# Performer attention with a hard-swish layer on one core: bfloat16 transposes for the second batch, another load order, and another rank for the first batch's second half

## The chip, the cores and the metric

The kernel runs on one core of one Trainium2 chip. The metric is device time in microseconds. The core has five engines that run side by side, each with its own stream of instructions: TensorE (PE in the profile; its weight loads are PEld), VectorE (DVE), ScalarE (ACT), GpSimd (POOL) and SyncE (SP), which here only issues transfers. Engines wait for each other through semaphores.

## The reference

Eight batches of eight heads with 576 tokens of width 64 go through an attention with random features, and its result through a two-layer network with a hard-swish gate.

```
def phi(x):
    proj = einsum('bhsd,md->bhsm', x, omega)
    sq = sum(x * x, axis=-1) / 2
    h = proj - sq
    h = h - max(h, axis=-1)
    return exp(h) / sqrt(m)
q_p, k_p = phi(q * scale), phi(k * scale)
kv  = einsum('bhsm,bhsd->bhmd', k_p, v)
z   = sum(k_p, axis=2)
num = einsum('bhsm,bhmd->bhsd', q_p, kv)
den = einsum('bhsm,bhm->bhs', q_p, z) + 1e-06
x   = (num / den)            # 4608 tokens x 512
h   = x @ w_in               # 512 -> 2048
g   = h * clip(h + 3, 0, 6) / 6
out = g @ w_out              # 2048 -> 512
```

The maximum is over the 128 features of each token. For q every factor that belongs to a token alone falls out of num / den. For k the factor 1 / max stays, and the kernel multiplies it into v.

## The kernel before

**Work of one batch.** A batch has four pairs of heads. Of the 576 tokens of a head, 512 are its main rows and 64 its leftover rows; all leftovers of a batch are handled together. For each batch, `attention(b)` does the following.

- `turns` transposes k and q in chunks of 128 x 128 on TensorE (operations `T`), and ScalarE or VectorE copies the result out of PSUM into `kT` and `qT` (`Tev`). This holds for batches 0 and 1 (`PE_T = 2`); later batches use DMA transposes issued by SP.
- `K`: TensorE projects k onto omega (L634), ScalarE takes the exponential (L640), VectorE the maximum over features (L643).
- `Q`: the same projection for q (L651) and exponential (L655), without a maximum.
- `pair(b, m, t)`: for a pair of heads VectorE takes the reciprocals (L735), VectorE or GpSimd multiplies v by them (`vc`, L739; `vcl`, L674, is the same for the leftover rows), TensorE forms `kv` (L752, L754), a copy brings it to SBUF as `kvz`, TensorE forms `num` (L775), VectorE divides (L787, L791).
- `turn_x` transposes the quotient (`X`) and copies it into `xT`, again on TensorE for batches 0 and 1 and by DMA for later ones. Batch 0 does this by halves of a pair (A and B), so that the first half of block 0 can begin early.

Block `blk` of the network is the 512 main tokens' worth of batch `blk`; a ninth block holds the leftovers of all batches (`xS`). `mm1` multiplies by `wi` (L843, for block 0 `mm1_half`, L868, in two halves A and B of tokens), ScalarE and VectorE form the gate (`relu`, L849 or L877; `g`, L851 or L879), and `mm2` multiplies by `wo` (L901). The `g` operation frees the PSUM bank.

**The two ways to transpose on TensorE.** The helper `turn` (L421) uses the transpose instruction with a bfloat16 result in PSUM for batch 0 (L423), and an ordinary matmul by the identity with a float32 result for batch 1 (L424). `turned` gives the view of the result, and the cost that the planner assumes for the copy is `both(n, 2)` for batch 0 and `both(n, 1)` for batch 1.

**What sets the order.** Operations are declared with a list of possible engines, an assumed duration, what they read and write, and a priority (smaller is sooner). `Prog.schedule` then plans all engines at once with these assumed durations: it picks an engine and a PSUM bank (eight banks, the ring) for each operation, and the order on each engine. `Prog.emit` writes the instructions in that order with the waits that remain. So a changed duration or priority can move instructions anywhere on any engine. `by_path` sets priorities: every operation that a goal depends on gets `base` minus 0.02 times its distance from the goal. It is called for the first matmuls of block 0's second half, `mm1.0B.0` (base -0.3), and then of its first half, `mm1.0A.0` (base -1.0). Since the operations of `mm1_half` are tied to each other in a chain by the key `"mm1"`, those of half A are among what `mm1.0B.0` depends on.

**Fillers.** While TensorE would have nothing to do at the start, the planner puts in matmuls on a constant tile (`idle`, L461).

**Loads.** Batch 0 is loaded in float32 (L495) by SP and ACT in the order of `FIRST`; ("k", 1) are k's main rows in four transfers, ("k", 0) its leftover rows in one. ScalarE, VectorE or GpSimd cast k and q to bfloat16. GpSimd issues the loads of w_in (L471) in four pieces, the first once the first piece of v has landed, and after them the loads of batch 1, w_out (L477), and so on; each of these is held back by a gate, an earlier transfer or a later matmul.

Of the kernel before, what the change touches and what calls it, by code (L numbers as in the profile page):

```python
# [41 lines left out]
class Prog:  # L42
# [8 lines left out]
    def op(self, eng, occ, emit, prio, reads=(), writes=(), alloc=(), lat=0.2, group=None, inc=1, name="", slack=0.0, dslack=0.0, issue=0.5, spare=0, packet=46.0):  # L51
        o = Op()
        o.engs = (eng,) if isinstance(eng, str) else tuple(eng)
        o.eng = None
        o.emit, o.occ, o.lat, o.prio, o.name = emit, occ, lat, prio, name
        o.alloc = list(alloc)
        o.group, o.inc, o.slack, o.dslack, o.issue, o.spare, o.packet = group, inc, slack, dslack, issue, spare, packet
        o.seq = len(self.ops)
        deps = {}
        virts = []  # L60
        for kx in reads:
            for d in self.w.get(kx, ()):
                deps[d] = True
            self.r.setdefault(kx, []).append(o)
            if isinstance(kx, Virt):
                virts.append(kx)
        for kx in writes:
            for d in self.r.get(kx, ()):
                if d is not o:
                    deps.setdefault(d, False)  # L70
            for d in self.w.get(kx, ()):
                deps.setdefault(d, False)
            self.w[kx] = [o]
            self.r[kx] = []
            if isinstance(kx, Virt):
                virts.append(kx)
        for vx in set(virts):
            vx.users.append(o)
            vx.left += 1
        o.virts = list(set(virts))  # L80
        o.deps = deps
        o.succ = []
        o.end = o.start = None
        o.emitted = None
        self.ops.append(o)
        return o

    def by_path(self, goals, base, scale):

        far = {o: 0.0 for o in goals}  # L90
        for o in reversed(self.ops):
            if o not in far:
                continue
            for d in o.deps:
                occ = min(d.occ.values()) if isinstance(d.occ, dict) else d.occ
                t = far[o] + occ + d.lat
                if t > far.get(d, -1.0):
                    far[d] = t
        for o, t in far.items():
            if o not in goals and o.prio > -8:  # L100
                o.prio = base - scale * t

    def schedule(self):
# [211 lines left out]
def _emit(nc, es, q, k, v, omega, w_in, w_out, out):  # L315
# [14 lines left out]
    HALVES = [(0, 2), (2, 4)]  # L330
    SPLIT = 3
    LATE = 0.4
    FIRST = [("k", 1), ("q", 1), ("k", 0), ("v", 0), ("v", 1), ("q", 0)]
    REST = [("k", 1), ("k", 0), ("q", 1), ("q", 0), ("v", 0), ("v", 1)]
    W_GATE = [("v32", 0, 1), ("v32", 0, 3), ("v32", 1, 3), ("v32", 1, 3)]
    alpha = float(D) ** -0.25
# [3 lines left out]
    EV_T = ("DVE", "ACT")  # L340
# [78 lines left out]
        return f  # L419

    def turn(E, vx, b, i, src):  # L421
        if b == 0:
            return E.transpose(ringb[vx.slot][:, 128 * i:128 * i + 128], src, ident[:])  # L423
        return E.matmul(ring.t[vx.slot][:, 128 * i:128 * i + 128], src, ident[:], start=True, stop=True)  # L424

    def turned(vx, b, n):
        return ringb[vx.slot][:, 0:n] if b == 0 else ring.t[vx.slot][:, 0:n]


    op("SP", 0.2, lambda E: E.dma_start(om32[:], omega), -9.8, writes=["om32"], group="dom", inc=16, lat=1.8,  # L430
# [109 lines left out]
    def attention(b):  # L540
# [30 lines left out]
        def turns(t, name, dbl, dst, src, p):  # L571
            vT = Virt(ring)
            n = 128 * len(dbl)

            def e_T(E):
                for i, x in enumerate(dbl):
                    ins = turn(E, vT, b, i, src[:, 2 * x:2 * x + 2, :].rearrange("p c d -> p (c d)"))
                return ins

            op("PE", len(dbl) * (0.057 if b else 0.06), e_T, p, reads=rows_of(t, dbl) + ["ident"],  # L580
               writes=[vT], alloc=[vT], lat=0.25, slack=sl, dslack=2 * sl, spare=sp, name="T%s%d.%s" % (t, b, name))
            op(EV_T if b else T0, both(n, 1 if b else 2), evac(lambda: dst, lambda: turned(vT, b, n).rearrange(
                "p (j t) -> p j t", j=dst.shape[1])),
               p, reads=[vT], writes=[(t + "T", x) for x in dbl], name="Tev%s%d.%s" % (t, b, name))

# [141 lines left out]
    def pair(b, m, t):  # L727
# [66 lines left out]
        def turn_x(i0, i1, part):  # L794
            vx = Virt(ring)
            n = 128 * (i1 - i0)
            pt = "" if len(part) > 1 else "AB"[part[0]]

            def e_x(E):
                for i in range(i0, i1):  # L800
                    ins = turn(E, vx, b, i - i0, xb[pb][:, m, 128 * i:128 * i + 128])
                return ins

            op("PE", (i1 - i0) * (0.057 if b else 0.06), e_x, t + 0.03, reads=[("xb", pb, m, x) for x in part] +
               ["ident"], writes=[vx], alloc=[vx], lat=0.25, slack=sl, spare=sp, name="X" + nm + pt)
            op(EV_T, both(n, 1 if b else 2), evac(lambda: xT[pb][:, m, 128 * i0:128 * i1], lambda: turned(vx, b, n)),
               t + 0.03, reads=[vx], writes=[("xT", pb, m, x) for x in part], name="Xev" + nm + pt)

        if b == 0:
# [189 lines left out]
```

## Time and profile before

| | us |
|---|---|
| median of five runs | 326.21 |
| lowest and highest | 325.78, 326.45 |
| the profiled execution | 325.78 |
| its span | 324.0 |
| TensorE busy in the span | 318.4 |
| VectorE, ScalarE, GpSimd busy | 208.6, 189.3, 78.5 |

How to read it: the span is the time between the first and the last instruction that the profiler saw. "Busy" counts an engine's instructions, fillers too. A timeline row gives the start, how long the row lasts, the engine, the line, the operation with its tiles and how many instructions the row holds; in brackets is the idle time of the engine before it and what ended that. A row of the waits gives the waiting engine and line, what it waited for, the total, the number of times and the longest one, in us. Matmuls overlap, so 42 of them take far less than 42 times the duration of one.

### The profile page before, as it was taken

The page shows a single profiled execution, that of the slowest core. Times are in us where ns is not written, and L with a number is a line of the kernel's source. Part 1 is how long each engine was busy: PE and PEld are TensorE (multiplying, and loading weights), DVE is VectorE, ACT ScalarE, POOL GpSimd, SP SyncE. Part 2 cuts the span into 40 slices and gives each one's busy share as a digit, 9 for nine tenths or more (in the row PEclk, how much of TensorE's full clock was granted, in tenths as well). Part 3 has the DMA queues.
Part 4 walks back from the last instruction along what each step waited for, and adds up shares of the span by engine and source line. Part 5 has one row for each costly group of instructions (what it writes and reads, how often), then busy time and mean ns, then how long its engine had stood idle before and what let it go on. Part 6 is the DMA issues. An engine that isn't in the chain of part 4 may idle for free.

```text
span 324.0 us, 5914 instructions
## 1 busy us (share of the span) xinstructions
PE 318.4 (98%) x2263; PEld 175.0 (54%) x2263; DVE 208.6 (64%) x463; ACT 189.3 (58%) x386; POOL 78.5 (24%) x110
## 2 busy tenths in 40 slices
PE   8999999999999999999999999999999999999996
PEld 6678865545554545555455545555555444444443
DVE  4869886698576938865687468756865354433411
ACT  3968981598387519755876377647674353444400
POOL 2725643057051502620244032402010000000000
PEclk9999999999999999999999999999999999999999
DMA  7999999989980999799629974996012201000024
GB/s 248 245 196 163 267 169 183 255 140 141 230 197 1 148 142 282 106 218 164 180 31 165 186 222 50 166 207 212 14 53 58 74 7 59 32 34 32 32 67 97
DMA packets 89516, 44.33 MB, mean 137 GB/s; under 512 B 56080, under 2 KB 85008, under 8 KB 89488
## 3 DMA queue, kind: packets, MB, share of 16 engines
q1 hardware_dynamic: 62272, 30.85, 42.0%
q0 software_dynamic: 26512, 12.46, 31.7%
q10 hardware_dynamic: 704, 0.66, 0.6%
q8 instruction: 18, 0.29, 0.4%
q14 instruction: 10, 0.08, 0.1%
HBM read 36.73 MB, written 9.44 MB: 143 GB/s over the span
## 4 chain that ended last, share of the span: by engine, by line
PE 93%; DVE 1%; issue 0%
PE p L901 38%; PE p L843 34%; PE p L651 4%; PE p L868 4%; PE p L634 4%; PE p L775 3%; PE p L752 2%; PE p L424 1%; PE p L754 1%; PE p L423 0%; DVE mx L643 0%; PE p L688 0%; DVE vc L739 0%; DVE xb L791 0%; DVE kvz L411 0%
## 5 line engine op out<-in xcount | busy, mean ns | idle before, releaser
L901 PE MATMUL p<-wo,gT 128*128 128x512 bf16 (+2 forms) x592 | 141.8, 373 | 0.0
L851 DVE SCALAR_TENSOR_TENSOR gT<-tsb,p 128x512 bf16<-128x512 bf16 x128 | 86.5, 683 | 53.4 <-ACT tsb L849 52.7
L849 ACT ACTIVATE tsb<-p 128x512 bf16<-128x512 f32 x128 | 76.9, 605 | 68.8 <-PE p L843 67.6
L843 PE MATMUL p<-xT,wi 128*128 128x512 bf16 x448 | 108.4, 379 | 0.0
L901 PEld LDWEIGHTS p<-wo,gT 128*128 128x128 bf16 x592 | 55.9, 98 | 55.5
L843 PEld LDWEIGHTS p<-xT,wi 128*128 128x128 bf16 x448 | 42.6, 98 | 45.4
L643 DVE TENSOR_REDUCE mx<-kp 128x4 f32<-128x512 bf16 x72 | 47.4, 675 | 15.5 <-ACT kp L640 15.3
L640 ACT ACTIVATE kp<-p 128x512 bf16<-128x512 f32 x72 | 40.9, 613 | 13.6 <-PE p L634 13.6
L655 ACT ACTIVATE qpT<-p 128x512 bf16<-128x512 f32 (+1 forms) x80 | 40.8, 579 | 3.3 <-PE p L651 3.3
L739 POOL TENSOR_TENSOR vc<-v,cc 128x512 bf16<-128x512 f32 x23 | 25.1, 1091 | 44.1 <-DVE cc L735 29.1
L791 DVE TENSOR_TENSOR xb<-p,rec 128x384 bf16<-128x384 f32 (+1 forms) x64 | 28.5, 476 | 0.0
L634 PE MATMUL p<-om,kT 128*128 128x256 bf16 x144 | 23.5, 273 | 0.1
L651 PE MATMUL p<-qT,om 128*128 128x512 bf16 (+1 forms) x80 | 22.9, 358 | 0.0
L410 ACT COPY osb<-p 128x512 f32<-128x512 f32 x26 | 15.3, 588 | 9.2 <-PE p L901 9.2
L674 POOL TENSOR_TENSOR vcl<-vl,cc 64x260 bf16<-64x260 f32 x8 | 5.0, 624 | 60.3 <-DVE cc L670 50.8
L411 DVE COPY osb<-p 128x512 f32<-128x512 f32 (+2 forms) x11 | 7.1, 643 | 18.7 <-PE p L901 18.7
L634 PEld LDWEIGHTS p<-om,kT 128*128 128x128 bf16 x144 | 13.2, 98 | 9.3 <-ACT kT L410 0.6
L775 PEld LDWEIGHTS p<-kvz,qpT 128*128 128x128 bf16 x312 | 13.9, 98 | 7.1 <-DVE kvz L411 0.6
L843 PE MATMUL p<-xS,wi 128*128 128x512 bf16 x64 | 16.4, 379 | 0.0
L752 PEld LDWEIGHTS p<-vc,kp 128*128 128x128 bf16 x256 | 12.0, 98 | 6.7 <-DVE vcl L674 0.5
L868 PE MATMUL p<-xT,wi 128*128 128x256 bf16 x128 | 15.6, 273 | 0.0
L775 PE MATMUL p<-kvz,qpT 128*128 128x65 bf16 x312 | 15.3, 194 | 0.1
(75 smaller groups left out, 223.9 us busy)
## 6 DMA issues: line engine op xcount, KB each, us to landing
out_dram<-osb SPq DMA_DIRECT2D x32, 256.0 KB, 2.7
v<-in_v_dram SPq DMA_DIRECT2D x14, 512.0 KB, 5.7
wi<-in_moe_w_in_dram POOLq DMA_DIRECT2D x4, 512.0 KB, 8.7
k<-in_k_dram POOLq DMA_DIRECT2D x8, 256.0 KB, 4.5
k<-in_q_dram POOLq DMA_DIRECT2D x8, 256.0 KB, 5.4
wo<-in_moe_w_out_dram POOLq DMA_DIRECT2D x4, 512.0 KB, 9.7
kb<-in_k_dram POOLq DMA_DIRECT2D x6, 256.0 KB, 5.3
qb<-in_q_dram POOLq DMA_DIRECT2D x6, 256.0 KB, 7.5
```

Source lines behind the costliest of these rows:

```text
L634: ins = E.matmul(ring.t[vK.slot][:, 256 * i:256 * i + 256], kT[:, 2 * u + i, :], om[:].rearrange("d t m -> d (t m)"), start=True, stop=True)
L640: op("ACT", actt(512), lambda E, u=u, vK=vK: E.activation(kp[pb][:, 4 * u:4 * u + 4, :].rearrange("p c m -> p (c m)"), ring.t[vK.slot], AF ...
L643: op("DVE", dvet(512), lambda E, u=u: E.reduce_max(mx[pb][:, 4 * u:4 * u + 4], kp[pb][:, 4 * u:4 * u + 4, :], axis=AX.X), pos(u) + 0.03, r ...
L651: op("PE", mmt(n), lambda E, vQ=vQ, lh=lh: E.matmul(ring.t[vQ.slot][:, 0:n], om[:, lh, :], src, start=True, stop=True), p + 0.045 * lh, re ...
L655: op("ACT", actt(n), lambda E, vQ=vQ, lh=lh: E.activation(dst(lh), ring.t[vQ.slot][:, 0:n].rearrange("m (j t) -> m j t", t=128), AF.Exp, s ...
L775: ins = E.matmul(d[:, hh, i - i0, :], qpT[pb][:, o:o + 128], kvz[m][:, 65 * hh:65 * hh + 65], start=True, stop=True)
L791: op("DVE", dvet(128 * n), lambda E: E.tensor_tensor(xv[:, :, i0:i1, :], psum()[:, :, :, 0:64], rbc, ALU.mult), t + 0.01, reads=[vn, ("rec ...
L843: ins = E.matmul(ring.t[vh.slot], wi[:, c, 128 * f:128 * f + 128], xv[:, c, :], start=(c == 0), stop=(c == NJ - 1))
L849: op("ACT", actt(512), lambda E: E.activation(tsb[tu][:], ring.t[vh.slot], AF.Relu, bias=0.5, scale=1.0 / 6.0), t - 0.1, reads=[vh], write ...
L851: op("DVE", dvet(512), lambda E: E.scalar_tensor_tensor(gT[gu][:, f, :], tsb[tu][:], 1.0, ring.t[vh.slot], ALU.min, ALU.mult), t - 0.1, re ...
L868: ins = E.matmul(ring.t[vh.slot][:, 256 * g:256 * g + 256], wi[:, c, 128 * (f + g):128 * (f + g) + 128], xT[0][:, c, 256 * half:256 * half ...
L901: ins = E.matmul(ring.t[vo.slot][:, 0:c1 - c0], gT[gu][:, f, 128 * tc:128 * tc + 128], wo[:, f, c0:c1], start=(f == 0), stop=(f == NF - 1))
```

## The change

Four edits, in three groups.

1. `turn` and `turned` lose their case for batch 1: all transposes on TensorE use the transpose instruction with a bfloat16 result. The planner's assumed durations follow (0.057 per transpose, the copy as fast as batch 0's).
2. In `FIRST`, k's leftover rows stand ahead of q's main rows.
3. `by_path` passes over operations whose name begins with `mm1`, so the matmuls of block 0's half A keep their own priorities (0 to 0.5), and all that leads to `mm1.0B.0` but is not an `mm1` has priorities below -0.3.

```
-            if o not in goals and o.prio > -8:
+            if o not in goals and o.prio > -8 and not o.name.startswith("mm1"):
                 o.prio = base - scale * t
...
-    FIRST = [("k", 1), ("q", 1), ("k", 0), ("v", 0), ("v", 1), ("q", 0)]
+    FIRST = [("k", 1), ("k", 0), ("q", 1), ("v", 0), ("v", 1), ("q", 0)]
...
     def turn(E, vx, b, i, src):
-        if b == 0:
-            return E.transpose(ringb[vx.slot][:, 128 * i:128 * i + 128], src, ident[:])
-        return E.matmul(ring.t[vx.slot][:, 128 * i:128 * i + 128], src, ident[:], start=True, stop=True)
+        return E.transpose(ringb[vx.slot][:, 128 * i:128 * i + 128], src, ident[:])

     def turned(vx, b, n):
-        return ringb[vx.slot][:, 0:n] if b == 0 else ring.t[vx.slot][:, 0:n]
+        return ringb[vx.slot][:, 0:n]
...
-            op("PE", len(dbl) * (0.057 if b else 0.06), e_T, p, reads=rows_of(t, dbl) + ["ident"],
+            op("PE", len(dbl) * 0.057, e_T, p, reads=rows_of(t, dbl) + ["ident"],
...
-            op(EV_T if b else T0, both(n, 1 if b else 2), evac(lambda: dst, lambda: turned(vT, b, n).rearrange(
+            op(EV_T if b else T0, both(n, 2), evac(lambda: dst, lambda: turned(vT, b, n).rearrange(
...
-            op("PE", (i1 - i0) * (0.057 if b else 0.06), e_x, t + 0.03, reads=[("xb", pb, m, x) for x in part] +
+            op("PE", (i1 - i0) * 0.057, e_x, t + 0.03, reads=[("xb", pb, m, x) for x in part] +
...
-            op(EV_T, both(n, 1 if b else 2), evac(lambda: xT[pb][:, m, 128 * i0:128 * i1], lambda: turned(vx, b, n)),
+            op(EV_T, both(n, 2), evac(lambda: xT[pb][:, m, 128 * i0:128 * i1], lambda: turned(vx, b, n)),
```

The planner's new order, read from the instructions that come out: TensorE has 59 fillers instead of 62 and otherwise the same matmuls. Before block 0's first matmuls stand eight more of batch 0's `num` matmuls and two more of its transposes. VectorE casts k's leftover rows right after its first copy of `kT`; ScalarE casts the piece of k that VectorE cast before; GpSimd instead of VectorE forms `vc` for pairs 0 and 2 and VectorE instead of GpSimd for pair 1; ScalarE instead of GpSimd casts q's leftover rows. On GpSimd `vc` of pair 0 stands between the first and the second w_in load, and `vc` of pairs 2 and 3 behind the fourth. Block 1's first seven `mm1` groups stand before batch 2's first K. On SP batch 3's v loads stand behind the two DMA transposes of its q. From batch 6's K projections on, TensorE's order is the same in both.

## The prediction

> **What bounds the kernel now.** I read the page first, then who waited on TensorE, then the engines' timelines of the first 45 us. The page's busy row and clock row:
>
> ```profile
> PE 318.4 (98%) x2263; PEld 175.0 (54%) x2263; DVE 208.6 (64%) x463; ACT 189.3 (58%) x386; POOL 78.5 (24%) x110
> ...
> PEclk9999999999999999999999999999999999999999
> ```
>
> TensorE is busy in all but 5.6 us of the 324.0, at full granted clock. The list of TensorE's waits is short:
>
> ```profile
> PE p L461 <- DVE fill L456: 1.3, 1, 1.3
> PE p L423 <- DVE xb L791: 0.4, 1, 0.4
> PE p L752 <- DVE vcl L674: 0.2, 1, 0.2
> PE p L423 <- DVE kb L411: 0.2, 1, 0.2
> ```
>
> So after 31 us nothing stops TensorE. But busy is not useful: 62 of its matmuls are fillers (L461), and TensorE's timeline shows where they stand:
>
> ```profile
> 14.10 1.36 PE L461 MATMUL p<-fill 128*128 128x256 bf16 x11
> 15.70 0.43 PE L752 MATMUL p<-vc,kp 128*128 128x65 bf16 x8 [0.23 <-DVE vcl L674]
> ...
> 19.08 0.42 PE L752 MATMUL p<-vc,kp 128*128 128x65 bf16 x8
> ...
> 20.94 0.83 PE L868 MATMUL p<-xT,wi 128*128 128x256 bf16 x6
> ...
> 26.77 1.91 PE L868 MATMUL p<-xT,wi 128*128 128x256 bf16 x16
> ...
> 29.77 0.28 PE L423 MATMUL p<-ident,xb 128*128 128x128 bf16 x2 [0.40 <-DVE xb L791]
> ```
>
> The last filler is at 17 us. The kv products start at 15.70 (pair 0) and 19.08 (pair 3), and block 0 at 20.94. Both kernels hold the same useful matmuls: only the fillers differ in number, 62 against 59. The time can therefore change only by the fillers and waits of the first 30 us, and by new waits later. The first kv waits for VectorE, the last for GpSimd:
>
> ```profile
> 14.74 0.91 DVE L674 TENSOR_TENSOR vcl<-vl,cc 64x260 bf16<-64x260 f32 x2
> ```
>
> ```profile
> 13.12 2.35 POOL L471 DMA_DIRECT2D wi<-in_moe_w_in_dram  x3 [0.19 <-issue]
> ...
> 17.88 1.04 POOL L739 TENSOR_TENSOR vc<-v,cc 128x512 bf16<-128x512 f32 x1 [0.81 <-DVE rec L787]
> 23.85 2.29 POOL L495 DMA_DIRECT2D k<-in_k_dram  x3 [4.93 <-DMA wi<-in_moe_w_in_dram]
> 26.36 2.72 POOL L495 DMA_DIRECT2D k<-in_q_dram  x4 [0.22 <-issue]
> ```
>
> The last two rows date w_in: their gates are its third and fourth pieces, landed by 23.85 and 26.36.
>
> **Part 1, k's leftover rows ahead of q.** One 128 KB load moves past four q loads on SP's queue. The q loads feed GpSimd's casts back to back (7.95, 9.52), so 256 KB take about 0.75 us; the leftover load has the bytes of half of one, and from its 256-byte pieces I take 0.6. It lands near 7.0 instead of 10.0 (cast at 10.02), and each q load 0.6 later; v's loads, behind both, do not move. q's cover: its casts end near 11.4 and the projections run between fillers at 13 to 14, so 0. In the new order ScalarE, not VectorE, casts one piece of k (0.54 as its copies run, 1.08 for two), GpSimd multiplies v for pair 0 instead of VectorE, and ScalarE casts q's leftovers instead of GpSimd.
>
> VectorE, with its own rows: kT's copies end near 9.05 (T of the last piece 8.2, two copies 0.75). Then seven maxima at 0.6 (1.23 for two), two reciprocals 0.2, both vcl 0.91: 9.05+4.2+0.2+0.9 = 14.35, against 15.65. ScalarE's nine exponentials (6 in 3.04) start near 7.75 and end at 12.3, ahead of the maxima. So kv of pair 0 starts at 14.4 instead of 15.70.
>
> GpSimd: pair 0's product is put between w_in's first and second issue, 12.58 to 13.62. The three remaining issues take 13.65 to 16.0, 0.5 late. Their landing: the first piece is still moving then (5.8 us is the shortest of the four from issue to landing, 11.62+5.8 = 17.4), so the transfers stay back to back; I take 0, at most 0.5. Queued behind these issues are pair 2's product, 16.0 to 17.05, and pair 3's, 17.05 to 18.1. So kv of pair 3 starts at 18.15, not 19.08: of the 1.3 us won, 0.9 survive GpSimd's queue.
>
> **Part 2, batch 0's second half ahead of block 0.** From pair 3's kv to its num was 0.86 us (19.08 to 19.94), from there to its division 0.86 (20.80), then 0.41 and 0.06 to the transposes: 18.15+2.19 = 20.34. The new order puts this transpose and a second-half num in front of block 0's first matmuls: 20.34+0.11+0.13 = 20.58 against 20.94, with some 0.5 us of idle ahead. From there to the first matmuls that need w_in's fourth piece: 48 matmuls at 0.109 (the chain of waits gives 4.58 us for 42), 8 nums 0.25, 8 transposes 0.45: 20.58+5.93 = 26.5, against 26.77. By then the new order has done more: 8 nums (0.25) and 8 transposes (0.45), less two q transposes (0.11): 0.59 us. And the 0.40 wait at 29.77 has its transposes far behind it: gone.
>
> Sum: (26.5-26.77) - 0.59 - 0.40 = **-1.26 us**. The ends: w_in's fourth piece, in between 26.1 and 26.4, stops any further gain at -1.65. If GpSimd's queue slips by the 0.5 it is pushed, -0.75.
>
> VectorE must hold block 0's first g until four more divisions are done (4 x 0.38, 4 reciprocals 0.5), near 22.8. At 0.66 each it then meets TensorE's 0.87 per group, so no bank runs out: 0, at most 0.4.
>
> **Part 3, batch 1's transposes in bfloat16.** 52 on TensorE, and the by-shape groups show the price of turning and emptying:
>
> ```profile
> L424 PE MATMUL p<-ident,k 128*128 128x128 bf16 x36 | 2.9, 219 | 0.0
> ...
> L423 PE MATMUL p<-ident,qb 128*128 128x128 bf16 x18 | 1.7, 219 | 0.0
> ...
> L411 DVE COPY kT<-p 128x512 bf16<-128x512 bf16 x3 | 1.2, 420 | 1.6 <-PE p L423 1.6
> ...
> L410 ACT COPY kT<-p 128x512 bf16<-128x512 bf16 x1 | 0.6, 586 | 3.6 <-PE p L423 3.6
> ...
> L411 DVE CAST kT<-p 128x512 bf16<-128x512 f32 x1 | 0.7, 679 | 0.0
> ```
>
> TensorE: 219 ns either way, 0. VectorE: 0.26 less for each of five 512-wide copies, ScalarE 0.1 for its seven: some 2 us together, around 30 to 58, where ScalarE is the busier. TensorE did not wait there before, so the path gains 0; the cover is real, though. Being earlier, TensorE meets w_out sooner: 40.1 for its first piece, which lands at 32.73+7.1 = 39.8. Margin 0.2; bounds 0 to +0.4, I take 0.
>
> A rule against the change: the Trainium skill, TensorE: Matmul & The Clock Gate, Part 4, says that transpose mode does not count as busy for the clock gate. Batch 0's transposes, already of that mode, run in a stretch whose granted clock reads 1.00. If the 52 then ran at half rate, an estimate from that page, each would take its 56 ns (0.22 us for 4) once more, and the sum would be 2.9 us worse. By the rows it is 0, and 0 is used.
>
> **Result.** The profiled execution took 325.78 for a span of 324.0, the lowest of five runs; the median is 326.21. From the profiled one the sum gives 324.5, from the median 325.0; I forecast the median at 325.1, with 0.1 for the margins above. No change that can be measured means within 0.2%, 325.6 to 326.9.
>
> **The rivals.**
> *The gain is handed back to a transfer.* TensorE, earlier, waits for w_out's pieces near 40 to 49, or for batch 3's v: the new SP order puts v behind two qT transposes that wait for q. For it: the margins of 0.2 and 0.4 us. Against: later pieces have about 1 us, and kv of batch 3 (near 92) has v's product about 2 us before. Price 0.5 to 1.3: 325.6 to 326.4.
>
> *ScalarE and VectorE jam at batch 2: slower.* Block 1's matmuls now begin before batch 2's K, so K and Q meet later groups of block 1:
>
> ```profile
> 60.00:80.00 20.00, 20.00 (x150) 11.11 (x149) 17.70 (x37) 18.27 (x41) 10.14 (x13) 1.00 1.06 181
> ```
>
> ScalarE was busy 18.27 of 20 us there. In the new order 10 relus, 9 exponentials of k, 8 and 2 of q lie between about 64.6 and 79: at their pace (0.545, 0.507, 0.515, 0.35) 14.8 us for 14.4. At their full durations (605, 613, 623, 401 ns) 17.4: three us over, and with eight banks TensorE would stop for most of it. It decides once the stop is over 1.9 us, which eats the 1.26 and another 0.65; with stops of 1.9 to 3 us the time is 326.9 to 328. Against it: the rows in runs show the pace.
>
> *The start does not shift*, because GpSimd's queue eats it all: pair 3's product would still begin at 17.9. Then only the 0.40 goes: 325.8 to 326.2.
>
> **How the numbers follow.** Forecast 0.62 (its own range 324.4 to 325.5), transfer rival 0.17, jam 0.15, no shift 0.06. Faster by over 0.2%: 0.62 and a third of the transfer rival's weight, where it takes little, 0.67. Slower: the jam and a little of worse transfers, 0.17. Same: 0.16. The range takes the forecast's low end, 324.4, and reaches up to 327.0, part of the jam; some 0.12 lies above and 0.06 below.
>
> **What would show it.** kv of pair 0 near 14.4 and of pair 3 near 18.15; block 0 near 20.6; w_in's fourth-piece matmuls at 26.5, with a wait for w_in at most 0.1; no wait at the second-half transposes; VectorE's copies of batch 1 at about 420 ns. Wrong if TensorE's list of waits has rows of several tenths after 31 us: at wo, at vc of batch 3, or at ScalarE between 64 and 80.

## The result, and the profile after

The changed kernel takes 325.7 us in the median of 53 runs, the kernel before 326.34 in the median of 95 (runs of several chips). The ratio is 0.9974 with a 95% interval of 0.9963 to 0.9986: faster by 0.26%, or 0.85 us. The profiled execution took 325.31 for a span of 323.5 us, against 325.78 and 324.0. Here and in the table of experiments a median counts every execution, while a ratio leaves out those over 1.5% slower than the fastest, so the two can differ.

TensorE's list of waits after the change (us in all, times, longest):

```profile
PE p L459 <- DVE fill L454: 1.3, 1, 1.3
PE p L866 <- DVE gT L877: 0.6, 1, 0.6
PE p L422 <- DVE kb L411: 0.4, 1, 0.4
PE p L422 <- POOL qb L411: 0.2, 1, 0.2
PE p L422 <- DVE xb L789: 0.2, 1, 0.2
```

The row of L866 is new. The wait of 0.40 us at 29.77, and the one for `vcl`, are gone. TensorE's timeline (start, duration, what, in brackets the idle time before it and what ended it; lines stand two lower than before from L424 on) shows the places that the prediction named:

```profile
14.37 0.43 PE L750 MATMUL p<-vc,kp 128*128 128x65 bf16 x8
...
18.12 0.43 PE L750 MATMUL p<-vc,kp 128*128 128x65 bf16 x8
...
20.57 0.82 PE L866 MATMUL p<-xT,wi 128*128 128x256 bf16 x6
...
23.67 3.00 PE L866 MATMUL p<-xT,wi 128*128 128x256 bf16 x26
27.24 1.03 PE L866 MATMUL p<-xT,wi 128*128 128x256 bf16 x8 [0.57 <-DVE gT L877]
...
43.37 0.22 PE L752 MATMUL p<-vcl,kp 128*128 128x130 bf16 x1
43.64 1.04 PE L899 MATMUL p<-wo,gT 128*128 128x512 bf16 x4
```

The start is where it was forecast: 14.37, 18.12 and 20.57. The stop at 27.24 is new. The row names VectorE's `gT`, but those eight matmuls are also the first that need w_in's fourth piece. The records of landings put the last part of that piece at 27.10 us (26.08 before); GpSimd's timeline shows it too, since its next load waits for it:

```profile
12.52 1.06 POOL L737 TENSOR_TENSOR vc<-v,cc 128x512 bf16<-128x512 f32 x1
13.50 2.31 POOL L469 DMA_DIRECT2D wi<-in_moe_w_in_dram  x3
15.81 2.25 POOL L737 TENSOR_TENSOR vc<-v,cc 128x512 bf16<-128x512 f32 x2
23.53 2.30 POOL L493 DMA_DIRECT2D k<-in_k_dram  x3 [5.47 <-DMA wi<-in_moe_w_in_dram]
27.39 2.73 POOL L493 DMA_DIRECT2D k<-in_q_dram  x4 [1.55 <-DMA wi<-in_moe_w_in_dram]
33.73 2.99 POOL L475 DMA_DIRECT2D wo<-in_moe_w_out_dram  x4 [3.61 <-DMA k<-in_q_dram]
```

The third piece is there by 23.53 (23.85 before), the fourth by 27.10. In all seven profiled executions with this stop (this one, and those called again, gates, gates2, f32copies, norank and firstalone below) the matmul starts 0.13 to 0.14 us after the piece's last part, also where the row names `gT`; so it is w_in that TensorE waits for. Everything queued behind the piece on GpSimd is late too: w_out is issued at 33.73 instead of 32.73. The chain of waits leads through both:

```profile
15.05 12.05 DMA wi<-in_moe_w_in_dram
28.12 5.33 DMA k<-in_q_dram
34.47 9.12 DMA wo<-in_moe_w_out_dram
43.64 1.04 PE p L899 x4
```

w_out's second piece ends at 34.47+9.12 = 43.59, and the matmuls behind it start at 43.64; 0.06 behind the row at 43.37, as elsewhere, they would have started at 43.43. So the second stop is 0.21 us. Idle by idle, the book closes: -1.26 forecast, +0.57 at w_in, +0.21 at w_out make -0.48; the spans differ by 0.5. (Idle time is counted from the end of the last matmul, which overlaps the next. By the starts, with 26 matmuls at 0.109 us from 23.67 on, TensorE was ready for the fourth piece at 26.50 and lost 0.74; the old wait of 0.40 cost 0.57 by the same count. The two differences of 0.17 cancel.)

After 44 us TensorE has no idle row. The stretch where one rival expected a jam (columns: stretch, length, busy time of PE, PEld, DVE, ACT, POOL with instructions, granted clock, DMA share, GB/s):

```profile
70.00:80.00 10.00, 10.00 (x61) 4.91 (x58) 9.30 (x21) 10.00 (x24) 6.36 (x8) 1.00 1.42 210
```

ScalarE is busy for all ten microseconds, and so is TensorE: the jam is that near, and it did not happen.

### The profile page after: what moved, and what is told of

Same layout as the page of the kernel before. It is cut to its first block, busy times and chain, and to the rows that moved or that the text cites. A ratio compares the mean times of both kernels' runs of the same rounds, so it can differ in the third digit from the quotient of the medians.

```text
span 323.5 us, 5896 instructions
## 1 busy us (share of the span) xinstructions
PE 317.6 (98%) x2260; PEld 174.7 (54%) x2260; DVE 209.5 (65%) x464; ACT 191.0 (59%) x388; POOL 78.0 (24%) x107
## 3 DMA queue, kind: packets, MB, share of 16 engines
q0 software_dynamic: 26512, 12.46, 31.1%
## 4 chain that ended last, share of the span: by engine, by line
PE 86%; DMA 10%; POOL 2%; SPq 1%; issue 1%; DVE 0%
PE p L899 38%; PE p L841 34%; PE p L649 4%; PE p L632 4%; DMA wi<-in_moe_w_in_dram 4%; DMA wo<-in_moe_w_out_dram 3%; PE p L773 3%; PE p L750 2%; DMA q<-in_q_dram 2%; DMA k<-in_q_dram 2%; SPq L493 1%; POOL wi L469 1%; PE p L752 0%; POOL qb L411 0%; POOL vc L737 0%
## 5 line engine op out<-in xcount | busy, mean ns | idle before, releaser
L638 ACT ACTIVATE kp<-p 128x512 bf16<-128x512 f32 x72 | 41.7, 619 | 14.3 <-PE p L632 14.2
L653 ACT ACTIVATE qpT<-p 128x512 bf16<-128x512 f32 (+1 forms) x80 | 42.5, 577 | 3.5 <-PE p L649 3.3
L632 PE MATMUL p<-om,kT 128*128 128x256 bf16 x144 | 24.4, 273 | 0.0
L649 PE MATMUL p<-qT,om 128*128 128x512 bf16 (+1 forms) x80 | 24.1, 358 | 0.0
L672 POOL TENSOR_TENSOR vcl<-vl,cc 64x260 bf16<-64x260 f32 x9 | 5.7, 629 | 54.7 <-DVE cc L668 30.9
L866 PE MATMUL p<-xT,wi 128*128 128x256 bf16 x128 | 16.1, 272 | 0.6 <-DVE gT L877 0.6
L493 POOL DMA_DIRECT2D k<-in_k_dram x12 | 9.2, 777 | 27.9 <-PE p L632 14.1
```

The costliest lines, as they stand in the source:

```text
L632: ins = E.matmul(ring.t[vK.slot][:, 256 * i:256 * i + 256], kT[:, 2 * u + i, :], om[:].rearrange("d t m -> d (t m)"), start=True, stop=True)
L638: op("ACT", actt(512), lambda E, u=u, vK=vK: E.activation(kp[pb][:, 4 * u:4 * u + 4, :].rearrange("p c m -> p (c m)"), ring.t[vK.slot], AF ...
L649: op("PE", mmt(n), lambda E, vQ=vQ, lh=lh: E.matmul(ring.t[vQ.slot][:, 0:n], om[:, lh, :], src, start=True, stop=True), p + 0.045 * lh, re ...
L653: op("ACT", actt(n), lambda E, vQ=vQ, lh=lh: E.activation(dst(lh), ring.t[vQ.slot][:, 0:n].rearrange("m (j t) -> m j t", t=128), AF.Exp, s ...
```

## The experiments

Theory S: the gain is the start's, won by parts 1 and 2, and what is missing of 1.26 us was given back at w_in and w_out. Rival C: the start's gain is all given back, and the shorter copies and the planner's new costs win the 0.85. Parts 1, 2 and 3 are those of the prediction: k's leftover rows ahead of q (`FIRST`), batch 0's second half ahead of block 0 (`by_path`), the bfloat16 transposes. Every ratio is against the kernel before on the same chip.

| run | edit | median, us | before, us | ratio (95%) |
|---|---|---|---|---|
| again | none | 325.88 | 326.41 | 0.9970 (0.9943 to 0.9996) |
| nofirst | without part 1 | 327.49 | 326.41 | 1.0026 (0.9999 to 1.0054) |
| norank | without part 2 | 327.78 | 326.41 | 1.0020 (0.9992 to 1.0048) |
| nobf | without part 3 | 326.33 | 326.41 | 0.9992 (0.9975 to 1.0009) |
| firstalone | part 1 alone | 327.74 | 326.61 | 1.0007 (0.9980 to 1.0034) |
| f32copies | part 3's order, long copies | 326.11 | 326.72 | 0.9975 (0.9952 to 0.9997) |
| wide | half as many fillers, twice as wide | 326.22 | 326.72 | 0.9976 (0.9955 to 0.9998) |
| narrow | each filler as two halves | 326.12 | 326.72 | 0.9991 (0.9971 to 1.0011) |
| gates | k, q, w_out issued earlier | 325.19 | 326.72 | 0.9951 (0.9932 to 0.9969) |
| wi5 | w_in in five pieces | 325.60 | 326.61 | 0.9981 (0.9956 to 1.0005) |
| wi5gates | five pieces, k and q earlier | 325.53 | 326.61 | 0.9972 (0.9944 to 1.0000) |
| gates2 | k and q issued earlier | 324.76 | 326.61 | 0.9925 (0.9898 to 0.9953) |

### The changed kernel once more

> The changed kernel as it is, profiled once more. In its first profile w_in's fourth piece came to TensorE 0.57 us late, because one of its 16 parts landed 1.4 us after the other 15. Theory S (the gain is the start's: parts 1 and 2 together win 1.26 us, and what is missing of it is this wait and the 0.2 us that w_out then cost): the time is 0.5 to 1.2 us below the kernel before, whichever way the fourth piece falls. S-chance (the late part is chance): the fourth piece lands within 8.2 us of its predecessors' first issue, near 26.1, the wait at block 0's fourth-piece matmuls is 0.2 or less, and the span is 322.8 to 323.1. S-floor (the later issue of w_in's pieces behind GpSimd's product puts it there): the piece lands again at 26.6 or later, the wait is 0.4 to 0.7 and the span 323.4 to 323.7. Rival C (the gain is that of the shorter copies and of the planner's new costs, and the start's is all given back) expects the same here and differs in the next three.

Measured: span 323.3, 325.06 us in the profiled execution. TensorE's timeline of this run:

```profile
26.86 1.03 PE L866 MATMUL p<-xT,wi 128*128 128x256 bf16 x8 [0.48 <-DVE gT L877]
43.38 1.04 PE L899 MATMUL p<-wo,gT 128*128 128x512 bf16 x3 [0.17 <-DMA wo<-in_moe_w_out_dram]
```

Both stops are there again, 0.48 and 0.17. The fourth piece landed at 26.72, where S-floor had it, but fifteen of its sixteen parts were there by 25.68, so it was one part that was late and not the whole piece. The span lies between the two forecasts of S-chance and S-floor, nearer to S-floor. Its twelve executions reach from 324.23 to 326.74, so how much is given back varies from one to the next.

### One part undone at a time

Part 1 undone:

```
-    FIRST = [("k", 1), ("k", 0), ("q", 1), ("v", 0), ("v", 1), ("q", 0)]
+    FIRST = [("k", 1), ("q", 1), ("k", 0), ("v", 0), ("v", 1), ("q", 0)]
```

> Part 1 undone: k's leftover rows again behind q's four loads; parts 2 and 3 stay. Theory S: kv of pair 0 starts at 15.7 and of pair 3 near 19.1 again; with the second half of batch 0 ahead, block 0 starts near 21.5, its fourth-piece matmuls near 27.4, past the landing of w_in's fourth piece, so no wait there, and the 0.40 us wait for the second half's transposes is gone: 0.68 later, 0.59 more done, 0.40 saved, so 0.2 to 0.4 us below the kernel before, and about 0.3 us above the changed kernel. Rival C (the copies): the same time as the changed kernel to 0.1 us, 0.8 us below before. Rival P (part 1 alone carries it): no gain at all, 0 to 0.3 us above before.

Measured: 0.26% above before, where theory S expected a gain of 0.2 to 0.4 us. TensorE's timeline:

```profile
15.51 0.43 PE L750 MATMUL p<-vc,kp 128*128 128x65 bf16 x8 [0.28 <-DVE vcl L672]
...
21.20 0.82 PE L866 MATMUL p<-xT,wi 128*128 128x256 bf16 x6
...
30.32 0.73 PE L422 MATMUL p<-ident,k 128*128 128x128 bf16 x10 [0.37 <-DVE gT L877]
...
46.07 1.04 PE L899 MATMUL p<-wo,gT 128*128 128x512 bf16 x4 [1.01 <-DMA wo<-in_moe_w_out_dram]
```

The start is the old one, and no wait for w_in, as expected. What was not expected lies later: 0.37 for VectorE's `g`, and 1.01 for w_out's third piece. That piece landed at 46.03 (44.78 before), though w_out was issued only 0.37 later than before. Three fillers more than before make up most of the rest. A reading that no run shows: part 2 puts useful work in front of block 0's matmuls, and with the old start that work is not there when TensorE meets w_out. Rival C falls: the copies and the new costs are in this kernel, and the gain is not.

Part 2 undone:

```
-            if o not in goals and o.prio > -8 and not o.name.startswith("mm1"):
+            if o not in goals and o.prio > -8:
```

> Part 2 undone: the second half of batch 0 ranked behind block 0's matmuls again; parts 1 and 3 stay. Theory S: the kv products start at 14.4 and 18.15, block 0 near 20.2; its fourth-piece matmuls would be reached near 26.1, so w_in's fourth piece stops them for as long as it is late: 0 if it lands at 26.1, 0.6 at 26.7, 0.9 at 27.0; the 0.4 us wait near 29.8 for the second half stays. 0 to 0.6 us below the kernel before, so 0.2 to 0.8 above the changed kernel. Rival C (the copies): the same time as the changed kernel to 0.1 us.

```profile
20.10 0.83 PE L866 MATMUL p<-xT,wi 128*128 128x256 bf16 x6
...
24.51 1.92 PE L866 MATMUL p<-xT,wi 128*128 128x256 bf16 x16 [0.38 <-DMA wi<-in_moe_w_in_dram]
...
27.67 1.03 PE L866 MATMUL p<-xT,wi 128*128 128x256 bf16 x8 [0.99 <-DMA wi<-in_moe_w_in_dram]
...
31.33 0.94 PE L866 MATMUL p<-xT,wi 128*128 128x256 bf16 x7 [0.73 <-ACT xT L410]
```

Block 0 starts at 20.10, earlier than in the changed kernel, and stands for w_in at the third piece and again at the fourth; then it stands 0.73 us for the second half's transposes, the old wait. The time is above before, not 0 to 0.6 us below: the price of w_in was larger than expected (1.37 in place of 0 to 0.9), because in this execution one part of the first piece landed 2.1 us behind the rest, and the later pieces kept about 1 us of it. Ten of its twelve executions spread from 325.4 to 328.8. That the early start is worth nothing without other work to put before w_in's landing held.

Part 3 undone, in the instructions and in the planner's costs (the lines that the change took out of `turn`, `turned` and the assumed durations come back):

> Part 3 undone: batch 1's transposes go back to matmuls against the identity with float32 results; parts 1 and 2 stay. Theory S: the copies of 512 columns on VectorE take 0.68 instead of 0.42 us, TensorE does not wait for them, and the time is that of the changed kernel to 0.2 us, 0.6 to 1.0 us below the kernel before. Rival C (the copies): the gain is gone, within 0.2 us of the kernel before. Rival T (transposes in their own mode cost TensorE clock): the time is up to 2.9 us below the changed kernel's.

The gain shrinks to 0.08% with an interval across 0, nearer to what rival C expected (that of before) than to S (that of the changed kernel); but the interval overlaps the changed kernel's (0.9963 to 0.9986), so the loss is not clear of noise. The profile shows a place for it, in TensorE's timeline:

```profile
59.01 0.39 PE L424 MATMUL p<-ident,xb 128*128 128x128 bf16 x4
...
60.56 2.76 PE L843 MATMUL p<-xT,wi 128*128 128x512 bf16 x12 [1.04 <-DVE xT L411]
```

Here the last transposes of batch 1's quotient stand directly in front of block 1's first matmuls, which need them. In the changed kernel (TensorE's timeline of it) they stand one group of w_out's matmuls earlier, and nothing is lost:

```profile
58.07 0.39 PE L422 MATMUL p<-ident,xb 128*128 128x128 bf16 x4
...
58.41 1.03 PE L899 MATMUL p<-wo,gT 128*128 128x512 bf16 x4
59.27 6.21 PE L841 MATMUL p<-xT,wi 128*128 128x512 bf16 x28
```

Two readings are left: the copies are too long, or the planner's other order puts them too late. The next run keeps the order and lengthens the copies.

```
-        return E.transpose(ringb[vx.slot][:, 128 * i:128 * i + 128], src, ident[:])
+        if b == 0:
+            return E.transpose(ringb[vx.slot][:, 128 * i:128 * i + 128], src, ident[:])
+        return E.matmul(ring.t[vx.slot][:, 128 * i:128 * i + 128], src, ident[:], start=True, stop=True)
...
-        return ringb[vx.slot][:, 0:n]
+        return ringb[vx.slot][:, 0:n] if b == 0 else ring.t[vx.slot][:, 0:n]
```

> The changed kernel with its order kept instruction by instruction (the planner still counts with short copies), but batch 1's 52 transposes run as matmuls against the identity with float32 results. With part 3 undone in the planner too, the time was 0.45 us above the changed kernel and TensorE waited 1.04 us for VectorE's copy of x's last transposes at block 1's first matmuls. Theory K (the copies' length costs it): VectorE's 512-column copies of batch 1 take 0.68 instead of 0.42, and a wait of 0.3 to 1.0 us for them appears, at block 1's first matmuls or earlier; the time is 0.3 to 1.0 us above the changed kernel. Rival O (the other order that the planner makes of float32's costs loses it, not the copies): no such wait, and the time of the changed kernel to 0.2 us. Rival T (transposes in their own mode cost TensorE clock): the time falls below the changed kernel's, by up to 2.9 us.

The by-shape groups of this run on VectorE (in all, mean ns), and of the changed kernel:

```profile
L411 DVE CAST kT<-p 128x512 bf16<-128x512 f32 x2 | 1.3, 686 | 0.0
```

```profile
L411 DVE COPY kT<-p 128x512 bf16<-128x512 bf16 x5 | 2.0, 423 | 0.9 <-PE p L422 0.6
```

The copies are as long as meant, 686 against 423 ns, and the ratio is 0.9975, the changed kernel's 0.9974. No wait for a copy of x stands at block 1's first matmuls. So the long copies cost no time that these runs resolve, as rival O had it. That the order which the planner makes of the new costs carries part 3 rests on the 1.04 us above, one execution. TensorE's timeline of this execution has two waits for ScalarE that the changed kernel's profiles lack:

```profile
27.71 1.03 PE L868 MATMUL p<-xT,wi 128*128 128x256 bf16 x8 [1.24 <-DMA wi<-in_moe_w_in_dram]
42.09 1.02 PE L901 MATMUL p<-wo,gT 128*128 128x512 bf16 x4 [0.61 <-ACT qpT L655]
71.33 0.38 PE L651 MATMUL p<-qT,om 128*128 128x512 bf16 x1 [0.46 <-ACT kp L640]
```

ScalarE's own copies into `kT` of the same shape take 587 to 590 ns in both forms, so it is not they; whether the long copies on VectorE or w_in's 1.24 us brought these two waits about is open. The medians leave room for a few tenths. With that, theory S and rival C are both too simple: the gain is the start's, but parts 1 and 2 both have to be there for it to reach the end. For part 3 this is likely and not shown.

### Part 1 alone

The edit is the line of `FIRST`, in the kernel before.

> The kernel before with part 1 alone: k's leftover rows ahead of q. Theory S: kv of pair 0 starts at 14.4 and of pair 3 near 18.1 as with all three parts, so the loads alone bring the start forward; but block 0 begins with its matmuls, as with part 2 undone, stands at w_in near 24 to 28 us for 0.5 to 1.4 us, and the 0.4 to 0.7 us wait for the second half's transposes near 30 stays: the time is 0 to 1.5 us above the kernel before. Rival P (part 1 alone carries the gain): 0.5 to 1.0 us below before.

Measured: 1.0007 (0.9980 to 1.0034), no gain. TensorE's timeline:

```profile
14.60 0.42 PE L752 MATMUL p<-vc,kp 128*128 128x65 bf16 x8
...
17.90 0.43 PE L752 MATMUL p<-vc,kp 128*128 128x65 bf16 x8
...
25.87 1.03 PE L868 MATMUL p<-xT,wi 128*128 128x256 bf16 x8 [0.29 <-DVE gT L879]
...
29.54 1.05 PE L868 MATMUL p<-xT,wi 128*128 128x256 bf16 x8 [0.71 <-ACT xT L410]
```

The loads alone bring the start forward, to 14.60 and 17.90, and the time does not fall: w_in takes 0.29, less than the 0.5 expected, and the second half's transposes 0.71. Rival P falls.

### Why w_in's fourth piece is late

Each piece lands in 16 parts. The trace's records of their landings show how far the last part is behind the fourteenth, in us. The records of packets on the page's queue q8 (18 loads of instructions, 16 KB each) give the load that falls nearest to the fourth piece. That they are TensorE's is inferred from their number (TensorE has 2260 matmuls and as many weight loads) and from how they move in the two runs below. Times count from the start of the span, as in the timelines; in the expectation for `wide` the same loads stand 0.06 to 0.2 us earlier.

| run | 3rd piece: last part behind by | 4th piece: behind by | load: start, duration | 14th part of 4th piece |
|---|---|---|---|---|
| before | 0.79 | 0.70 | 24.85, 0.96 | 25.38 |
| changed kernel | 0.08 | 1.40 | 24.96, 0.96 | 25.70 |
| again | 0.35 | 1.06 | 24.68, 0.96 | 25.66 |
| f32copies | 0.96 | 2.07 | 25.23, 0.96 | 25.50 |
| gates2 | 0.65 | 1.10 | 25.05, 0.96 | 26.01 |
| norank | 1.03 | 1.36 | 25.52, 0.96 | 26.17 |
| nobf | 0.80 | 0.70 | 24.56, 0.96 | 25.05 |
| firstalone | 0.76 | 0.80 | 24.54, 0.96 | 24.93 |
| gates | 1.36 | 1.30 | 25.75, 0.96 | 26.60 |
| wide | 0.47 | 0.55 | 25.51, 0.96 | 26.67 |
| nofirst | 0.23 | 0.23 | 26.10, 0.96 | 25.27 |

In five of the ten rows in which the load lies inside the piece, the last part falls behind by a further 0.3 to 1.3 us there; in the other five it was 0.5 to 1.4 behind already and stays so. In nofirst, where the load comes after the piece, nothing is added. Nor is it in wi5 (below): its load, at 24.54, lies inside the last of five pieces, and the last part goes from 0.30 to 0.40 behind. The five rows suggest a theory L: the load holds one DMA engine for about a microsecond, and the part of the piece on that engine lands as much later. Two runs moved the load by the number of TensorE's instructions ahead of it. In the first, the helper takes the fillers' width as a new argument:

```
-            idle_work(IDLE[1], 0.11, [("k32", 0, 0)])
+            idle_work(IDLE[1], 0.22, [("k32", 0, 0)], 512)
```

> The changed kernel with the fillers after k's arrival at 512 columns instead of 256, half as many: the useful work and its order stay, but TensorE has issued 23 matmuls fewer by 20 us. The records of TensorE's program loads (16 KB each, about 1 us on one DMA engine) stand at 24.9 and 24.5 us in the two profiles of the changed kernel, inside w_in's fourth piece, and only one part of 16 of that piece came late, by 1.4 and 1.05 us; without part 1 the load came at 25.9, after the piece, and no part was late. Theory L (the program load holds one DMA engine and makes w_in's last part late): the load moves some 2 to 3 us later, behind the fourth piece, which lands at 25.5 to 26.2; the wait at its matmuls falls from 0.5 to at most 0.1, the span to 322.6 to 323.0, the time by 0.4 to 0.7 us below the changed kernel, 1.2 to 1.5 below before. S-chance (the late part has nothing to do with it): a late part and a wait of 0.4 to 0.6 as in both profiles so far, and the time of the changed kernel to 0.2 us.

Inconclusive. The load stood at 25.51, still inside the piece, and in this execution the whole start came 0.9 us later (GpSimd issued w_in at 12.46 instead of 11.56), so that TensorE came to w_in after it had landed; w_out then stopped it twice, for 1.2 us in all. The ratio is the changed kernel's.

```
-            op("PE", each, lambda E, vw=vw: E.matmul(ring.t[vw.slot][:, 0:256], fill[:, 0:128], fill[:, 128:384],
-                                                     start=True, stop=True),
+            def two(E, vw=vw):
+                E.matmul(ring.t[vw.slot][:, 0:128], fill[:, 0:128], fill[:, 128:256], start=True, stop=True)
+                return E.matmul(ring.t[vw.slot][:, 128:256], fill[:, 0:128], fill[:, 256:384], start=True, stop=True)
+
+            op("PE", each, two,
```

> The opposite of the wide fillers: each filler as two matmuls of 128 columns, in the same place and as long in all, so that TensorE has issued some 59 matmuls more by 20 us and its program loads come earlier. Theory L: the load that stood at 24.9 us comes at 17 to 20 us, while w_in's second or third piece moves; one part of that piece is late by about 1 us and, the pieces following each other without a gap, one part of each later piece too, the fourth landing 0.3 to 1.0 us behind its other parts, but no new delay starts in the fourth: time within 0.3 us of the changed kernel. S-chance: the late part starts in any piece, wherever the load stands.

The load moved to 21.90, into the third piece (its 14th part lands at 22.97). The third piece's last part is 0.98 behind, after 0.28 in the second; the fourth's 0.65: a new delay in the third, none in the fourth, as theory L had it, and no wait for w_in. In its place TensorE waited for k of batch 1, one of whose late parts it met (timeline):

```profile
32.39 0.73 PE L422 MATMUL p<-ident,k 128*128 128x128 bf16 x10 [1.51 <-DMA k<-in_k_dram]
```

The ratio, 0.9991, is no better than the changed kernel's. So nofirst and narrow fit theory L, but of the twelve loads that lie inside a second or later piece (narrow and wi5 included) six bring no further delay, and delays of up to 2.5 us also arise in first pieces (2.50 us in gates, 2.11 in norank, 0.03 in before), with another such load near 13 us in all three, so the load alone does not say when a part is late. The records don't tell which DMA engine carried a part, so a rival stays untested: that it is always the same one or two engines, whatever the load does. L is suggested, not shown; that a late part is the cause of the stop is shown by the landings.

### Taking the two stops away

Gates on GpSimd's queue: k of batch 1 after w_in's second piece, q after its third, w_out after k.

```
-            load(1, (), {"k": [("wi", 2)], "q": [("wi", 3)], "v": [("kb", 1, 16)]})
+            load(1, (), {"k": [("wi", 1)], "q": [("wi", 2)], "v": [("kb", 1, 16)]})
-            for g, key in enumerate((("qb", 1, 16),("qb", 1, 16),("qb", 1, 16),("qb", 1, 16))):
+            for g, key in enumerate((("kb", 1, 16),("kb", 1, 16),("kb", 1, 16),("kb", 1, 16))):
```

> The changed kernel with three gates on GpSimd's queue opened earlier: batch 1's k is issued once w_in's second piece has landed (instead of the third), q once the third has (instead of the fourth), and w_out once k of batch 1 has landed (instead of q). Theory S: w_in keeps its place ahead in the queue, so its fourth piece and the wait for it stay (0 to 0.6 us); w_out's issue moves from 33.7 to about 30, its second piece lands by 41 instead of 43.5 and TensorE's 0.2 us wait near 43.4 goes: the time is 0.2 us below the changed kernel. Rival (the DMA engines share among what is issued): k's transfer beside w_in's last two pieces makes the fourth later by 0.5 us or more, the wait grows to 1 us or more, and the time is 0.5 to 1.0 us above the changed kernel.

0.9951 (0.9932 to 0.9969), the median 1.5 us below before. The profiled execution was the slowest of its thirteen, 329.88 us, and shows what this edit risks (TensorE's timeline):

```profile
28.04 1.03 PE L866 MATMUL p<-xT,wi 128*128 128x256 bf16 x8 [0.62 <-DVE gT L877]
45.91 0.42 PE L750 MATMUL p<-vc,kp 128*128 128x65 bf16 x8 [2.16 <-POOL vc L737]
```

w_in's stop stays, w_out's is gone, and v of batch 1, which now moves beside w_out and lands at 44.09 instead of 38.03, stops TensorE for 2.16 us. That is not all it cost: from 46.66 on TensorE's granted clock is 0.50 for 3.41 us, half of which, 1.7 us, is lost as well. The other twelve executions took 324.06 to 326.18, so this is one loss in thirteen and not the run's usual time. So w_out goes back behind q, and only k's and q's gates stay (the first pair of lines of the diff above):

> Only batch 1's k and q issued one piece of w_in earlier; w_in in four pieces and w_out behind q, as in the changed kernel. In the run with w_out issued behind k, w_in's wait was 0.6 us as ever, w_out no longer stopped TensorE, the median was 1.5 us below before, and one execution lost 2.2 us to batch 1's v, which moved beside w_out. Theory S: the wait for w_in stays at 0 to 0.6, w_out's wait of 0.2 goes, v is not held up: 0.2 to 0.4 us below the changed kernel, and no wait for v's product near 46. Rival (w_out's early issue was what won there): the time of the changed kernel to 0.15 us.

0.9925 (0.9898 to 0.9953), 324.76 us: faster than the changed kernel, whose interval (0.9963 to 0.9986) lies above it. TensorE's timeline:

```profile
27.25 1.03 PE L866 MATMUL p<-xT,wi 128*128 128x256 bf16 x8 [0.43 <-DMA wi<-in_moe_w_in_dram]
...
43.38 0.22 PE L752 MATMUL p<-vcl,kp 128*128 128x130 bf16 x1
43.43 1.02 PE L899 MATMUL p<-wo,gT 128*128 128x512 bf16 x4
```

The same place as in the changed kernel, 0.05 instead of 0.27 us behind the row at 43.38: w_out is there, and v holds up nothing. The wait for w_in stays, and now the row names it. S expected 0.2 to 0.4 us; the measured gain over the changed kernel is 0.9 us by the medians and 1.6 us by the ratios. The profile (span 323.3) explains the 0.2 alone; with six timed executions, the rest may be their draw, and no run shows another cause.

The other stop: w_in's last piece in two halves.

```
-    WI = [(0, 4), (4, 8), (8, 12), (12, 16)]
+    WI = [(0, 4), (4, 8), (8, 12), (12, 14), (14, 16)]
...
-    W_GATE = [("v32", 0, 1), ("v32", 0, 3), ("v32", 1, 3), ("v32", 1, 3)]
+    W_GATE = [("v32", 0, 1), ("v32", 0, 3), ("v32", 1, 3), ("v32", 1, 3), ("wi", 0)]
```

> The changed kernel with w_in's last piece cut in two halves (five pieces, 512, 512, 512, 256, 256 KB); q of batch 1 waits for the fifth. The first half needs 1.27 us less to land, and 8 matmuls of it (0.87 us) stand before the first that need the second half. Theory S (w_in's last bytes are the floor under the start): a last part that is late by 0.5 to 1.4 us, as in the changed kernel's profiles, is now covered by some 0.9 us, so TensorE waits 0 to 0.3 us for w_in instead of 0.5, and the time is 0.2 to 0.5 us below the changed kernel, 1.0 to 1.3 below before. Rival (the gain is not held by w_in but by w_out or later): the wait for w_in goes and the same amount comes back at w_out between 40 and 47 us, with the time of the changed kernel to 0.15 us. Rival V (VectorE, which now multiplies v for pair 3, becomes late): kv of pair 3 starts 0.3 us or more after 18.1, and the time is 0.2 us or more above.

0.9981 (0.9956 to 1.0005): no gain over the changed kernel. The timeline of the engines together:

```profile
17.55 0.81 POOL L469 DMA_DIRECT2D wi<-in_moe_w_in_dram  x1 [0.98 <-PE p L649]
...
18.37 0.25 POOL L742 TENSOR_TENSOR vc<-ones,cc 128x8 bf16<-128x8 f32 x1
18.67 0.43 PE L750 MATMUL p<-vc,kp 128*128 128x65 bf16 x8 [1.08 <-POOL vc L742]
```

The fifth issue waits on GpSimd for its gate, the first piece's landing (the row names TensorE; the same row of the next run, held 1.51 us, names w_in); a small product of pair 3 is queued behind it, and TensorE stands 1.08 us for that before block 0 begins. This is rival V's place, by GpSimd's queue and not by VectorE. TensorE then comes 1 us later to w_in and finds it landed, so whether the halves cover a late part was not put to the test.

> The five pieces of w_in, and batch 1's k and q issued one piece of w_in earlier than in the changed kernel (k after the second, q after the third), w_out behind q as before. Theory S: both stops that took the gain back, w_in near 27 and w_out near 43, are smaller: q of batch 1 lands 0.5 to 1 us earlier, w_out is issued near 33 instead of 33.7, no wait at w_out over 0.1 us; the full 1.26 us of the start are kept, 0.4 to 0.7 us below the changed kernel. Rival: batch 1's k moves beside w_in's last pieces and delays them; the wait for w_in grows to 0.5 us or more and the time is not below the changed kernel's.

The same stop, longer: 1.66 us in the profiled execution, and 0.9972 (0.9944 to 1.0000). After it, from 20.43 on, the granted clock is again 0.50 for 3.41 us; this execution took 327.01, and only one other of the twelve has a mean granted clock below 0.999, so the median of 325.53 does not hold that loss. Here, too, no wait for w_in or w_out, and nothing gained over the changed kernel.

## Why the prediction was right, and where its sum was not

The class was right: faster, by 0.26%, with the time of 325.7 inside the range. The point, 325.1, was 0.6 us too low. 325.7 lies outside the forecast's own range (324.4 to 325.5) and just inside that of the first rival, the gain handed back to a transfer (325.6 to 326.4); the stated range held it because it was wide enough for the rivals. The sign "a wait for w_in at most 0.1" failed. So the mechanism of the start was right, but how much of its gain was left depended on how late a part of w_in came, which changes from one execution to the next and which the prediction had priced at 0; that enough was left is in part luck.

- **Part 1.** Right to 0.05 us: kv of pair 0 at 14.37 (14.4), of pair 3 at 18.12 (18.15), block 0 at 20.57 (20.58). GpSimd's queue held pair 3's product behind the three issues (2.31 us), as priced.
- **w_in's fourth piece.** This is the term that was mis-sized: "the transfers stay back to back; I take 0, at most 0.5". From the second piece on they did stay back to back (third piece 23.53), and the fourteenth part of the fourth came 0.32 us later than before; but its last part was late by itself, 1.40 us behind where before it was 0.70. Together that is the 1.02 us from 26.08 to 27.10. The idle time was 0.57; in other executions of this order it was 0.48 (again), 0.43 (gates2), 0.62 (gates) and 1.24 (f32copies), and none in wide and narrow, where the piece was there first. The landing was read off one execution of the kernel before, in which TensorE came at 26.77; brought to 26.50, as forecast, nothing was left to absorb a late part.
- **w_out's first piece, "margin 0.2; bounds 0 to +0.4, I take 0".** 0.21 was lost, at the second piece. The margin was worked out with w_out's old issue time; but that issue hangs on w_in's fourth piece through q's load, so the two delays are one: 1.0 us at the issue.
- **Part 2.** The 0.59 us of work brought forward and the wait of 0.40 that goes are in the profile. The sum added the parts; the runs show that they do not add. Part 1 alone gains nothing (1.0007), nor do parts 2 and 3 without it (1.0026), nor parts 1 and 3 without part 2 (1.0020); a loss in the last two is likely, but their intervals reach just below 1.
- **Part 3, "the path gains 0".** Right for what it priced: transposes 219 to 220 ns in either form, VectorE's copies 423 ns against 679, and no difference in time that the runs resolve with long copies in the same order. What it left out is the planner's new costs for them: without these the last transposes of batch 1 stand in front of block 1, and in the one profiled execution 1.04 us are lost there. The rule on the clock gate (the Trainium skill, TensorE: Matmul & The Clock Gate, Part 4), that transposes do not count as busy, would by the prediction's estimate have made the sum 2.9 us worse; the stretch from 28 to 60 us, with all 52 transposes among other matmuls, ran at a granted clock of 1.00, and undoing part 3 made nothing faster.
- **The jam rival** was near, with ScalarE busy for 10.00 of 10 us, and no stop came of it. That the start does not shift is refuted by pair 3's kv at 18.12 (19.08 before).

## What to carry to other kernels

When a change brings the start of a chain forward, look up the next transfer that the chain meets and the spread of its last part over several executions, not its landing in one; a margin of a few tenths counts as none. A load that is issued behind a gate hands any delay of the earlier load on to the later one, so two stops at two weights can be one cause, and the cheap repair is at the gate. An edit's new cost in a planner is a change of its own: run it apart from the instruction that it describes.

## What the runs showed of the hardware that was not expected

One or two of the sixteen parts of a 512 KB transfer landed up to 2.5 us after the rest, while the pieces of w_in followed each other every 2.5 to 2.7 us from the second on; whoever waits for the transfer waits for the last part (27.10 us for the matmuls at 27.24). Within an unbroken stream the delay stays with the later pieces (0.90, 0.79, 0.70 in the second to fourth piece of the kernel before). Loads of the program itself, 16 KB and about 1 us each, stand among the DMA packets, and in six of the twelve cases looked at such a delay grew in the piece during which one of them moved.

A stop of TensorE can cost more than its length. After 2.16 us (gates) and 1.66 us (wi5gates) of standing still the granted clock was 0.50 for 3.41 us; after 1.51 us (narrow), 1.24 us (f32copies) and 1.08 us (wi5) it stayed at 1.00.
